# A Fourier mixing layer and two MLPs: where seven weight conversions and the split of x are placed

## The chip, the core and the metric

The kernel runs on one core of a Trainium2 chip. The metric is the device time of one execution in microseconds (us), lower is better. The inputs are float32 in HBM, and the output is float32.

## The reference, cut to what matters

```python
X = np.fft.rfft(x, axis=1)                       # x: (2, 3008, 256)
Yr = Xr @ w_r - Xi @ w_i + b_r                   # complex mixing, 256 x 256
Yi = Xr @ w_i + Xi @ w_r + b_i
Yr = np.sign(Yr) * np.maximum(np.abs(Yr) - 0.01, 0.0)   # and Yi
y = np.fft.irfft(Y, n=3008, axis=1).astype(np.float32)
for w_in, w_out, act in ((w_in1, w_out1, gelu_sigmoid), (w_in2, w_out2, silu)):
    y = act(y.reshape(6016, 256) @ w_in) @ w_out        # 256 x 2048, 2048 x 256
```

The weights of the two MLPs arrive as 64-bit patterns of doubles (the kernel reads them as int64) and have to be turned into float32 on the chip.

## The kernel before

The program has four stages that PE runs one after the other: the forward transform (16 groups of float32 matmuls, L344), the mixing (12 units, L496 to L502), the inverse transform (16 steps of float32 matmuls, L344 again) and the two MLPs (L727 and L755). Below, the units of the mixing are counted from 0 to 11: unit i is one (batch, parity, block), and its input x is two tiles of 128x512, `xt...0` and `xt...1` (cosine and sine part).

**The mixing.** Units 0 and 1 (`n32` is 2) use float32 matmuls. Units 2 to 11 are split: x is written as a high part `xh` (float32r, a CAST on ACT) and a low part `xl`, and each product takes three passes (high with high weight, high with low weight, low with high weight), 24 matmuls and one for the bias. The low part is made by ACT (it writes -x rounded, L476) and by a DMA that POOL issues and that adds x to it in place (L477). `xsplit` makes both parts, several units ahead. After a unit, `mid_post` (L506 on) copies a PSUM bank with ACT (`us`), adds and subtracts on DVE (`sd`), thresholds on ACT and DVE (`th`), and `mid_fold` makes the tiles `f` that the inverse reads, on DVE and POOL (`f`, `fb`, `fd`).

**A conversion** of a block of MLP weights goes through the engines in turn: a DMA of SP brings the raw bits into the one buffer `raw64`; ACT takes an absolute value (`cv_c`, L165); DVE does five steps (L170 to L174); a DMA that POOL issues adds `cv_c` to `cv_a` (L227; 256 KB); then the block is placed: for `wi` blocks DVE makes four sums `tmp` (L202 to L205), ACT casts two high parts (L99) and POOL subtracts two low parts (L100); for `wo` blocks one cast and one subtraction. `tick` does the next link of this chain for the next block, at the places that the lists `tf` (forward), `tm` (mixing) and `ti` (inverse) name. There are two buffers `cv_a`.

**What sets the order.** In the forward stage POOL and SP follow the written order, in the mixing SP, in the inverse PE; a scheduler orders the other engines' instructions at build time. Each engine then takes its list strictly in that order, and an instruction that waits holds up all behind it.

**Memory.** The `xt` slots (14 and 12) hold x and, once x is read, the tiles `f`. The pool `nh` on the left holds 8 low and 6 high parts. The pool `wib0` for weight blocks 4 and 5 (`wi4`, `wi5`) is opened on the left only after `nh` and `wh` are closed, at the end of the mixing.

```python
for i in range(N('n32') + 4):
    xsplit(i, 1)
    if i < N('n32') + 3:
        xsplit(i, 0)
for i in range(len(mids)):
    ps = mid_mm(i)
    if i >= N('n32'):
        xsplit(i + 4, 1)
        xsplit(i + 3, 0)
```

Of the kernel before, what the change touches and what calls it, by code (L numbers as in the profile page):

```python
# [21 lines left out]
P = 128  # L22
# [34 lines left out]
def spectral_mlp_kernel(ctx, tc, xin, mfwd, minv, wc, bias, w_in1, w_out1, w_in2, w_out2, outT):  # L57
# [360 lines left out]
    load_m()  # L418
    for g in range(3, N('fa')):
        fold(g)  # L420
    prev = None
    for g, (q, b, t) in enumerate(groups):
        fold(g + N('fa'))
        ps = fwd_mm(g)
        if b == B - 1 and m_order[0][0] == "f":
            load_m()
        if prev is not None:
            fwd_evac(*prev)
        prev = (g, ps)
        if g == 6:  # L430
            closed("lv0")
            wc_p = opened("wc", "right")
            wc_s = wc_p.tile([P, 2, 3 * D], F32, name="wc_s")
            bias_hl = wc_p.tile([P, 2 * D], F32R, name="bias_hl")
            bias_lo = wc_p.tile([1, 2 * D], F32R, name="bias_lo")
            bias_f = wc_p.tile([P, 2 * D], F32, name="bias_f")
            nc.gpsimd.memset(bias_f, 0.0)
            ones = wc_p.tile([P, P], F32R, name="ones")
            ones_f = wc_p.tile([P, P], F32, name="ones_f")

            neglam = wc_p.tile([P, 1], F32, name='neglam')
# [24 lines left out]
    xsp = {}

    def xsplit(i, part):
        if not N('n32') <= i < len(mids):
            return  # L470
        b, p, j = mids[i]
        for cs in range(2):
            x = xt[b, p, j, cs].rearrange("p q m c -> p (q m c)")
            if part:
                t = nh_p.tile([P, 512], F32R, tag="lo", name="xl", bufs=8)
                nc.scalar.mul(t, x, -1.0)  # L476
                nc.gpsimd.dma_start(out=t, in_=x, accum_op=ALU.add)  # L477
            else:
                t = nh_p.tile([P, 512], F32R, tag="hi", name="xh")
                nc.scalar.copy(t, x)  # L480
            xsp[b, p, j, cs, part] = t[:, :].rearrange("p (q m c) -> p q m c", q=2, m=2)
# [553 lines left out]
```

## Time and profile before

| | |
|---|---|
| median of 3 runs | 1181.35 us (1181.19 to 1182.56) |
| the profiled execution | 1181.88 us, of which its span is 1179.8 us |
| PE busy | 1157.4 us, 98% of the span |
| DVE, ACT, POOL busy | 632.7, 761.3, 499.9 us |
| mixing on PE | 67.3 to 140.4 us of the span |
| inverse on PE | 140.4 to 197.6 us |

PE is nearly always busy, so what a change can give or take lies in PE's few waits. The share of busy time hides them: they are read from PE's timeline, and what ended each of them from the names behind the arrow.

### The profile page before, as it was taken

The numbers are of one execution on the slowest core, as the hardware profiler recorded it, in microseconds if no ns is written. First come the engines' busy times: TensorE is split into PE (matmuls) and PEld (weight loads), VectorE is DVE, ScalarE is ACT, GpSimd is POOL, SyncE is SP. The second block draws the span as 40 slices with busy tenths as digits, with TensorE's granted clock in tenths as the row PEclk, the third lists the DMA queues.
The fourth block names the chain that finished last, engine by engine and source line by source line (L and its number), as shares of the span: only waits on it lengthen the run. The fifth ranks groups of instructions, "written<-read, shape, count | busy, mean of one in ns | idle before, by whom it ended". The sixth has DMA issues, their size and how long they took to land.

```text
span 1179.8 us, 14452 instructions
## 1 busy us (share of the span) xinstructions
PE 1157.4 (98%) x5036; PEld 940.4 (80%) x5036; DVE 632.7 (54%) x976; ACT 761.3 (65%) x1437; POOL 499.9 (42%) x421
## 2 busy tenths in 40 slices
PE   7999989999999999999999999999999999999998
PEld 4758866788888888888889978878888888888897
DVE  7857998666456465565564553432532623524422
ACT  2465633678667667677667776666765765766655
POOL 2353532454444444444436755333333333433333
PEclk9999999999999999999999999999999999999999
DMA  7568332231221221121120100000000000000000
GB/s 267 181 135 229 54 72 54 55 80 28 54 72 36 54 72 28 45 72 37 54 63 28 54 18 19 1 37 1 1 37 1 20 17 1 36 1 1 36 1 32
DMA packets 33610, 61.35 MB, mean 52 GB/s; under 512 B 3073, under 2 KB 12289, under 8 KB 33538
## 3 DMA queue, kind: packets, MB, share of 16 engines
q1 hardware_dynamic: 25730, 46.28, 11.6%
q0 software_dynamic: 7808, 14.16, 6.9%
q8 instruction: 39, 0.64, 0.2%
q14 instruction: 33, 0.27, 0.1%
HBM read 35.92 MB, written 10.35 MB: 39 GB/s over the span
## 4 chain that ended last, share of the span: by engine, by line
PE 72%; ACT 5%; DVE 2%; issue 1%; DMA 0%; POOL 0%; DVEq 0%; ACTq 0%; POOLq 0%
PE o L727 38%; PE x L755 34%; ACT yt L758 2%; ACT g L760 1%; ACT x L674 1%; DVE x L681 1%; ACT yt L774 0%; DVE yt L776 0%; DVE yt L731 0%; DVE yt L797 0%; ACT yt L791 0%; DMA cv_a<-cv_c 0%; ACT yt L789 0%; ACT yt L731 0%; ACT wi L99 0%
## 5 line engine op out<-in xcount | busy, mean ns | idle before, releaser
L765 POOL TENSOR_TENSOR g<-yt,g 128x512 fp32r<-128x512 f32 (+1 forms) x282 | 361.3, 1294 | 531.6 <-PE x L755 364.3
L727 PE MATMUL o<-g,wo 128*128 128x512 f32 (+1 forms) x2304 | 561.0, 386 | 0.9 <-POOL g L765 0.9
L755 PE MATMUL x<-x,wi 128*128 128x512 f32 (+1 forms) x2016 | 501.7, 387 | 5.4 <-ACT yt L791 2.0
L727 PEld LDWEIGHTS o<-g,wo 128*128 128x128 f32 x2304 | 432.4, 188 | 83.6 <-POOL g L765 1.2
L755 PEld LDWEIGHTS x<-x,wi 128*128 128x128 f32 x2016 | 376.0, 188 | 86.0 <-ACT yt L774 5.6
L758 ACT ACTIVATE yt<-yt 128x512 f32<-128x512 f32 (+1 forms) x288 | 179.1, 622 | 257.8 <-DVE yt L797 209.9
L760 ACT CAST g<-yt 128x512 fp32r<-128x512 f32 (+1 forms) x384 | 234.4, 612 | 11.8
L797 DVE TENSOR_TENSOR yt<-yt,x 128x512 f32<-128x512 f32 (+1 forms) x96 | 64.7, 674 | 212.9 <-PE x L755 212.6
L776 DVE TENSOR_TENSOR yt<-yt,x 128x512 f32<-128x512 f32 (+1 forms) x96 | 64.8, 675 | 168.7 <-ACT yt L774 165.9
L765 DVE TENSOR_TENSOR g<-yt,g 128x512 fp32r<-128x512 f32 (+1 forms) x102 | 72.7, 713 | 77.8 <-ACT g L760 77.8
L344 PE MATMUL psf<-m,xf 128*128 128x376 f32 (+2 forms) x208 | 61.1, 456 | 6.4 <-DVE xf L303 6.1
L681 DVE TENSOR_TENSOR x<-yt,x 128x512 fp32r<-128x512 f32 (+1 forms) x46 | 47.8, 1038 | 36.1 <-ACT x L674 36.1
L800 DVE TENSOR_TENSOR yt<-yt,x 128x512 f32<-128x512 f32 (+1 forms) x96 | 64.7, 674 | 0.0
L344 PEld LDWEIGHTS psf<-m,xf 128*128 128x128 f32 x208 | 39.2, 199 | 27.6 <-DVE xf L303 7.3
L774 ACT COPY yt<-x 128x512 f32<-128x512 f32 (+1 forms) x96 | 54.7, 570 | 5.9 <-issue 3.6
L758 ACT ACTIVATE yt<-x 128x512 f32<-128x512 f32 (+1 forms) x96 | 56.1, 584 | 2.1 <-PE x L755 2.1
L344 PE MATMUL psi<-m,f 128*128 128x376 f32 (+3 forms) x208 | 52.1, 406 | 4.3 <-DVE rt L374 4.3
L791 ACT COPY yt<-x 128x512 f32<-128x512 f32 (+1 forms) x96 | 55.8, 581 | 0.8 <-PE x L755 0.8
L789 ACT COPY yt<-x 128x512 f32<-128x512 f32 (+1 forms) x96 | 54.8, 571 | 0.8 <-PE x L755 0.8
L344 PEld LDWEIGHTS psi<-m,f 128*128 128x128 f32 x208 | 37.2, 194 | 17.8 <-DVE rt L374 5.5
L227 POOL DMA_DIRECT2D cv_a<-cv_c x32 | 27.8, 870 | 24.7 <-DVE cv_c L174 14.2
L384 ACT COPY xt<-psf 128x128 f32<-128x128 f32 (+2 forms) x96 | 18.6, 282 | 28.6 <-PE psf L344 28.5
(99 smaller groups left out, 817.8 us busy)
## 6 DMA issues: line engine op xcount, KB each, us to landing
raw<-in_wi SPq DMA_DIRECT2D x32, 256.0 KB, 3.2
cv_a<-cv_c POOLq DMA_DIRECT2D x32, 256.0 KB, 3.3
raw<-in_wo SPq DMA_DIRECT2D x16, 512.0 KB, 3.4
raw<-in_x SPq DMA_DIRECT2D x12, 512.0 KB, 4.8
xl<-xt POOLq DMA_DIRECT2D x20, 256.0 KB, 7.6
out_t<-yt SPq DMA_DIRECT2D x20, 256.0 KB, 2.0
m<-in_mf SPq DMA_DIRECT2D x4, 564.0 KB, 5.3
m<-in_mi SPq DMA_DIRECT2D x4, 564.0 KB, 10.5
```

The source lines that it names most:

```text
L344: nc.tensor.matmul(ps, hi[:, c : c + P], m[:, k, :w], start=i == 0, stop=i == last)
L681: E('xl1' if l else 'xl0' if i == 0 else 'xl', k).tensor_sub(lo, src, r32(hi))
L727: nc.tensor.matmul(acc[h, mm], st, mv, start=first and k == 0, stop=last and k == 2)
L755: nc.tensor.matmul(ps, st, mv, start=first and m == 0, stop=m == 2, skip_group_check=True)
L758: nc.scalar.activation(g, g if src is None else src, func)
L760: nc.scalar.copy(gh, g)
L765: eng.tensor_sub(gl, g, r32(gh))
L776: nc.vector.tensor_add(y1, y1, Y)
L789: nc.scalar.copy(y2, Z)
L791: nc.scalar.copy(y3, X)
L797: nc.vector.tensor_add(y2, y2, X)
L800: nc.vector.tensor_add(y3, y3, Z)
```

## The change

It does four things. The ticks of the mixing go from units 2, 6, 10 to units 1, 4, 7, 10 and those of the inverse from steps 1, 4, 7, 10 to 2, 5, 8. High parts of x are put into the `xt` slots, so that `nh` keeps low parts alone, 6 of them where 8 were. `wib0` is opened at the start of the mixing. The low parts of unit 2 get two tiles of their own in the pool `wc` and are made in the forward stage; those of the other units are made three units ahead, where it was four.

```diff
-'tm': [2, 6, 10], 'ti': [1, 4, 7, 10]
+'tm': [1, 4, 7, 10], 'ti': [2, 5, 8]
...
+    def xsplit(i, part, pool=None):
...
+            if part:
+                t = pool.tile([P, 512], F32R, tag="lo", name="xl", bufs=2 if pool is wc_p else None)
+                nc.scalar.mul(t, x, -1.0)
+                nc.gpsimd.dma_start(out=t, in_=x, accum_op=ALU.add)
+            else:
+                t = slot(cs, F32R, "xh")
+                nc.scalar.copy(t, x)
...
         if g == 13:
             prep_wc()
+            xsplit(N('n32'), 1, wc_p)
...
     mid_p = opened("mid", "right", 2)
     ft = {}
+    wib_p.append(opened("wib0", "left", 2))
     wh_p = opened("wh", "left")
-    nh_p = opened("nh", "left", N('nhb'))
+    nh_p = opened("nh", "left", 6)
...
-    for i in range(N('n32') + 4):
-        xsplit(i, 1)
-        if i < N('n32') + 3:
-            xsplit(i, 0)
+    for i in range(N('n32'), N('n32') + 3):
+        if i > N('n32'):
+            xsplit(i, 1, nh_p)
+        xsplit(i, 0)
     for i in range(len(mids)):
         ps = mid_mm(i)
         if i >= N('n32'):
-            xsplit(i + 4, 1)
+            xsplit(i + 3, 1, nh_p)
             xsplit(i + 3, 0)
...
     closed("mid", "wc", "nh", "wh")
-    wib_p.append(opened("wib0", "left", 2))
```

**The low parts of unit 6, on ACT.** The names: `us` is the copy of a unit's bank (`us_838` before and `us_835` now are unit 2's, `us_887` is unit 3's), `xt1000` and `xt1001` are x of unit 6, `wi4` is the fifth block. Before:

```order
L517 ACTIVATE th_770<-sd_766,neglam_379 128x512
L509 COPY us_838<-psm_723 128x512
L517 ACTIVATE th_770<-sd_766,neglam_379 128x512
L165 ACTIVATE cv_c_1227<-raw64_1030 128x512
L480 CAST xh_756<-xt0120_106 128x512
L476 ACTIVATE xl_750<-xt1000_108 128x512
L480 CAST xh_758<-xt0121_107 128x512
L476 ACTIVATE xl_753<-xt1001_109 128x512
L517 ACTIVATE th_844<-sd_840,neglam_379 128x512 x2
L509 COPY us_890<-psm_797 128x512
```

Now:

```order
L511 COPY us_835<-psm_742 128x512
L165 ACTIVATE cv_c_1088<-raw64_917 128x512
L436 CAST xh_879<-xt1010_110 128x512
L99 CAST wi4_1249<-cv_a_902 128x384
L99 CAST wi4_1249<-tmp_1250 128x512
L519 ACTIVATE th_841<-sd_837,neglam_379 128x512 x2
L511 COPY us_887<-psm_794 128x512
L432 ACTIVATE xl_821<-xt1000_108 128x512
L436 CAST xh_953<-xt1020_112 128x512
L436 CAST xh_881<-xt1011_111 128x512
L432 ACTIVATE xl_824<-xt1001_109 128x512
```

ACT reached `xl` of unit 6 before it turned to unit 2's thresholds (`th_844`); now it does so behind both casts of `wi4`, unit 2's thresholds (`th_841`) and unit 3's copy. Its tile is one that unit 3 reads, so it also waits for unit 3's matmuls.

**The DMAs of POOL for units 6 to 8.** Here `fd` is made of the folds of units 3 and 4. Before, from the DMA of the fifth conversion on:

```order
L227 DMA cv_a_1015<-cv_c_1014 128x512
L530 TENSOR_TENSOR f0011_836<-th_770 128x512
L477 DMA xl_750<-xt1000_108 128x512
L477 DMA xl_753<-xt1001_109 128x512
L477 DMA xl_824<-xt1010_110 128x512
L477 DMA xl_827<-xt1011_111 128x512
L227 DMA cv_a_1228<-cv_c_1227 128x512
L530 TENSOR_TENSOR f0101_940<-th_896 128x512
L477 DMA xl_876<-xt1020_112 128x512
L477 DMA xl_879<-xt1021_113 128x512
L536 TENSOR_TENSOR fd_995<-f0100_938,fb_993 128x512
```

Now, from the same place:

```order
L100 TENSOR_TENSOR wi4_1249<-tmp_1250,wi4_1249 128x512
L227 DMA cv_a_1089<-cv_c_1088 128x512
L433 DMA xl_821<-xt1000_108 128x512
L433 DMA xl_824<-xt1001_109 128x512
L100 TENSOR_TENSOR wi5_1387<-cv_a_1089,wi5_1387 128x384
L433 DMA xl_873<-xt1010_110 128x512
L433 DMA xl_876<-xt1011_111 128x512
L227 DMA cv_a_1252<-cv_c_1251 128x512
L100 TENSOR_TENSOR wi5_1387<-tmp_1388,wi5_1387 128x512
L532 TENSOR_TENSOR f0101_959<-th_893 128x512
L538 TENSOR_TENSOR fd_1014<-f0100_957,fb_1012 128x512
L433 DMA xl_947<-xt1020_112 128x512
```

Unit 6's low parts (`xt1000`, `xt1001`) left ahead of the sixth conversion's DMA and now leave behind it, and unit 8's (`xt1020`) left ahead of `fd` and now leave behind it.

**DVE in the inverse,** from one release of a PSUM bank that PE waits for (L374, batch 1, first step) to the next (L374, second step). Before:

```order
L374 TENSOR_TENSOR rt_1451<-psi_1401,eo_1452 128x4x94
L665 TENSOR_TENSOR yt_1325<-yt_1325 128x512
L627 TENSOR_TENSOR ac_1480<-rt_1451,psi_1456 128x377
L681 TENSOR_TENSOR x_1604<-tmp_1527,x_1603 128x512
L627 TENSOR_TENSOR ac_1480<-rt_1451,psi_1457 128x377
L619 TENSOR_TENSOR rt_1451<-psi_1441,eo_1466 128x2x2x95
L628 TENSOR_TENSOR rt_1451<-rt_1451,psi_1456 128x377
L683 TENSOR_TENSOR tmp_1527<-yt_1325,tmp_1527 128x512
L170 TENSOR_SCALAR cv_c_1489<-cv_c_1489 128x512
L628 TENSOR_TENSOR rt_1451<-rt_1451,psi_1457 128x377
L374 TENSOR_TENSOR rt_1451<-eo_1466,psi_1441 128x4x94
```

Now:

```order
L374 TENSOR_TENSOR rt_1451<-psi_1422,eo_1452 128x4x94
L666 TENSOR_TENSOR yt_1346<-yt_1346 128x512
L682 TENSOR_TENSOR x_1604<-tmp_1540,x_1603 128x512
L628 TENSOR_TENSOR ac_1494<-rt_1451,psi_1470 128x377
L684 TENSOR_TENSOR tmp_1540<-yt_1346,tmp_1540 128x512
L620 TENSOR_TENSOR rt_1451<-psi_1441,eo_1480 128x2x2x95
L629 TENSOR_TENSOR rt_1451<-rt_1451,psi_1470 128x377
L172 SCALAR_TENSOR_TENSOR cv_a_1461<-raw64_1405,cv_c_1460 128x512
L628 TENSOR_TENSOR ac_1494<-rt_1451,psi_1471 128x377
L374 TENSOR_TENSOR rt_1451<-eo_1480,psi_1441 128x4x94
```

Between the two releases stand eight steps where nine stood; ahead of the first of them, in the inverse, stood twelve more steps of conversions and sums, and now none.

## Rows read from the trace of the kernel before

**Rows 1.** Busy time by stretch: us, PE, PEld, DVE, ACT, POOL, granted clock, DMA share, GB/s.

```profile
83.60:140.40 56.80, 56.80 (x248) 46.62 (x249) 47.68 (x88) 35.51 (x62) 25.50 (x24) 1.00 0.73 165
140.40:163.10 22.70, 22.70 (x135) 21.60 (x133) 21.74 (x36) 8.01 (x15) 12.95 (x12) 1.00 0.17 41
...
167.80:171.40 3.60, 0.00 (x0) 0.00 (x0) 3.60 (x7) 2.15 (x4) 1.83 (x1) 1.00 0.19 34
171.40:175.70 4.30, 4.25 (x8) 2.37 (x9) 4.30 (x9) 0.00 (x0) 0.00 (x0) 0.62 0.00 0
```

**Rows 2.** PE's timeline: start, us, what; in brackets the wait and what ended it.

```profile
83.56 0.50 PE L499 MATMUL psm<-wh,xl 128*128 128x512 f32 x1 [1.46 <-DMA xl<-xt]
...
103.14 0.39 PE L502 MATMUL psm<-bias_hl,ones 128*128 128x512 f32 x1
...
108.85 0.39 PE L502 MATMUL psm<-bias_hl,ones 128*128 128x512 f32 x1
...
163.71 4.06 PE L344 MATMUL psi<-m,f 128*128 128x376 f32 x12 [0.59 <-DVE rt L374]
171.45 8.91 PE L344 MATMUL psi<-m,f 128*128 128x376 f32 x22 [3.68 <-DVE rt L374]
```

**Rows 3.** DVE's groups by line in the inverse, 140 to 198 us: the conversion's five steps.

```profile
L172 DVE SCALAR_TENSOR_TENSOR cv_a<-raw,cv_c 128x512 uint32<-128x512 uint32 x4 | 3.5, 879 | 0.0
L171 DVE TENSOR_SCALAR cv_c<-cv_c 128x512 uint32<-128x512 uint32 x3 | 2.8, 945 | 0.0
L174 DVE SCALAR_TENSOR_TENSOR cv_c<-raw,cv_c 128x512 f32<-128x512 uint32 x4 | 2.7, 683 | 0.0
...
L173 DVE TENSOR_SCALAR cv_c<-cv_a 128x512 uint32<-128x512 uint32 x4 | 2.5, 615 | 0.0
...
L170 DVE TENSOR_SCALAR cv_c<-cv_c 128x512 f32<-128x512 f32 x3 | 2.3, 782 | 1.0 <-ACT cv_c L165 1.0
```

**Rows 4.** ACT's timeline in the mixing: a raw block, units 2 and 3, unit 6's low part.

```profile
68.13 0.68 ACT L165 ACTIVATE cv_c<-raw 128x512 f32<-128x512 f32 x1 [3.60 <-DMA raw<-in_wi]
...
91.46 0.57 ACT L509 COPY us<-psm 128x512 f32<-128x512 f32 x1
...
95.09 0.63 ACT L476 ACTIVATE xl<-xt 128x512 fp32r<-128x512 f32 x1
...
100.90 0.57 ACT L509 COPY us<-psm 128x512 f32<-128x512 f32 x1
```

**Rows 5.** DVE's timeline in the mixing: conversions and the fold that `fd` waits for.

```profile
83.13 3.06 DVE L171 TENSOR_SCALAR cv_c<-cv_c 128x512 uint32<-128x512 uint32 x1
...
88.58 0.42 DVE L173 TENSOR_SCALAR cv_c<-cv_a 128x512 uint32<-128x512 uint32 x1
...
89.51 0.68 DVE L174 SCALAR_TENSOR_TENSOR cv_c<-raw,cv_c 128x512 f32<-128x512 uint32 x1
...
97.30 0.29 DVE L202 TENSOR_TENSOR tmp<-cv_a 128x128 f32<-128x128 f32 x1 [3.15 <-DMA cv_a<-cv_c]
...
115.63 0.69 DVE L530 TENSOR_TENSOR fb<-th 128x512 f32<-128x512 f32 x1
```

**Rows 6.** POOL's timeline in the mixing: weight steps, `fd`, and the low parts behind it.

```profile
83.26 1.40 POOL L100 TENSOR_TENSOR wi<-cv_a,wi 128x384 fp32r<-128x384 f32 x1
84.24 1.66 POOL L100 TENSOR_TENSOR wi<-tmp,wi 128x512 fp32r<-128x512 f32 x1
...
107.56 1.80 POOL L530 TENSOR_TENSOR f<-th 128x512 f32<-128x512 f32 x1 [1.44 <-DVE th L518]
...
116.41 1.68 POOL L536 TENSOR_TENSOR fd<-f,fb 128x512 f32<-128x512 f32 x1 [5.33 <-DVE fb L530]
```

**Rows 7.** DMA issues, KB each, us to landing; around 90.7, 96.0 and 118.0 us.

```profile
cv_a<-cv_c POOLq DMA_DIRECT2D x1, 256.0 KB, 6.5
...
xl<-xt POOLq DMA_DIRECT2D x1, 256.0 KB, 8.9
...
xl<-xt POOLq DMA_DIRECT2D x1, 256.0 KB, 3.8
```

More of the change, by code (lines that the diff above doesn't have):

```diff
@@ L10 @@
 F32 = mybir.dt.float32
-CFG = {'lv0': 'V', 'lv': 'VVVVVPVVVVVP', 'dd0': 'VPVVPPPPPVVP', 'dd': 'VVVVVVVVVVPV', 'ths': 'VVVVPV', 'thf': 'VVVP', 'ivf': 'VVVPVVVV', 'cva': 'P', 'pol': 'PPPP', 'pil': 'P', 'mvl': 'PVVP', 'xl': 'V', 'xse': 'V', 'gl': 'VPPPPPPP', 'tf': [6, 9, 12], 'tm': [2, 6, 10], 'ti': [1, 4, 7, 10], 'kb': [0, 1, 1, 1, 1, 1, 1, 0], 'kr': [0, 1, 0, 1, 0, 1, 1, 0], 'fa': 3, 'xp': [2, 4, 4, 5], 'xq': [1, 4, 1], 'xs': 4, 'xi': [11, 12, 13, 15], 'xsi': 9, 'ca': 4, 'tl': True, 'fwd': 'Pool,SP', 'rest0': 'all', 'rest1': 'all', 'last1': 'all', 'inv': 'PE', 'mid': 'SP', 'last0': 'all', 'thm': 'A', 'gl0': 'PVPVVVPV', 'gl2': 'PPPPPPPP', 'gl3': 'PPPPPPPV', 'xl0': 'V', 'xl1': 'V', 'pre': 14, 'pre2': 0, 'yd': 6, 'lvb': 6, 'mlp': 'none', 'pr': 'VVVP', 'pf': 'PV', 'eo': '0010', 'n32': 2, 'xa': 4, 'nhb': 6, 'ddb': 6, 'mlp1': 'all', 'mlp2': 'all'}
+CFG = {'lv0': 'V', 'lv': 'VVVVVPVVVVVP', 'dd0': 'VPVVPPPPPVVP', 'dd': 'VVVVVVVVVVPV', 'ths': 'VVVVPV', 'thf': 'VVVP', 'ivf': 'VVVPVVVV', 'cva': 'P', 'pol': 'PPPP', 'pil': 'P', 'mvl': 'PVVP', 'xl': 'V', 'xse': 'V', 'gl': 'VPPPPPPP', 'tf': [6, 9, 12], 'tm': [1, 4, 7, 10], 'ti': [2, 5, 8], 'kb': [0, 1, 1, 1, 1, 1, 1, 0], 'kr': [0, 1, 0, 1, 0, 1, 1, 0], 'fa': 3, 'xp': [2, 4, 4, 5], 'xq': [1, 4, 1], 'xs': 4, 'xi': [11, 12, 13, 15], 'xsi': 9, 'ca': 4, 'tl': True, 'fwd': 'Pool,SP', 'rest0': 'all', 'rest1': 'all', 'last1': 'all', 'inv': 'PE', 'mid': 'SP', 'last0': 'all', 'thm': 'A', 'gl0': 'PVPVVVPV', 'gl2': 'PPPPPPPP', 'gl3': 'PPPPPPPV', 'xl0': 'V', 'xl1': 'V', 'pre': 14, 'pre2': 0, 'yd': 6, 'lvb': 6, 'mlp': 'none', 'pr': 'VVVP', 'pf': 'PV', 'eo': '0010', 'n32': 2, 'xa': 4, 'nhb': 6, 'ddb': 6, 'mlp1': 'all', 'mlp2': 'all'}
 NUM = dict(li=[5, 6, 7, 8], n32=2, nhb=6, tf=[5, 9, 13], tm=[1, 3, 5, 7, 9, 11], ti=[0, 2, 4, 6, 8, 10, 12, 14, 14, 15, 15], kb=[2] * 8, kr=1, fa=3, fe=2, pm=0, nf=4, lvb=6, ddb=8, ivb=1, eob=1, fsb=6, f1=3, f2=0, fm=[7, 8, 9], fi=[1, 1, 2, 2], pre=13, pre2=1, yd=3, psh=0, ie=[12], xp=[1, 3, 4, 5], xq=[1, 2, 2], xs=5, nw=4, xi=[14, 14, 15, 15], xsi=13, rw=2, ca=4, cc=2, tb=1, tmn=1)
@@ L420, in spectral_mlp_kernel @@
         fold(g)
+    xsp = {}
+    mids = [(b, p, j) for b in range(B) for p in range(2) for j in range(NJ)]
+    def xsplit(i, part, pool=None):
+        if i >= len(mids):
+            return
+        b, p, j = mids[i]
+        for cs in range(2):
+            x = xt[b, p, j, cs].rearrange("p q m c -> p (q m c)")
+            if part:
[5 more added lines that the diff above has]
+                nc.scalar.copy(t, x)
+            xsp[b, p, j, cs, part] = t[:, :].rearrange("p (q m c) -> p q m c", q=2, m=2)
     prev = None
@@ L452, in spectral_mlp_kernel @@
             tick(N('tf').count(g))
-    mids = [(b, p, j) for b in range(B) for p in range(2) for j in range(NJ)]
     closed("xs", "lv", "raw", "m0")
@@ L465, in spectral_mlp_kernel @@
     nc.vector.tensor_sub(wl, wc_s, r32(wh))
[L466 to L481, printed above, removed]
     def mid_mm(i):
```

## The prediction

> **What bounds the kernel now.** I read the table by stretch first. In the mixing PE is busy for 56.80 of 56.80 us, in the first part of the inverse for 22.70 of 22.70 [rows 1]: PE is the bound, and a change pays only where PE waits. Then PE's timeline, for those waits. From the mixing to the end of the inverse there are three: 1.46 us for a DMA of low parts (unit 2's, the first split unit) and 0.59 and 3.68 us for DVE's release of a PSUM bank in the inverse [rows 2]. Then the granted clock. Behind the 3.6 us in which PE does nothing stands a stretch of 4.3 us with a mean of 0.62 [rows 1], so PE, at the lower of its two levels (1.2 GHz) for most of it, lost 0.38 x 4.3 = 1.6 us more. What makes DVE late there: it is busy for 21.74 of 22.70 us and then for every microsecond of the wait [rows 1], and 18 conversion steps, 13.8 us, are among its work in the inverse [rows 3].
>
> So the waits that the change can end come to 1.46 + 0.59 + 3.68 + 1.6 = 7.3 us, and with all of it and nothing against it the profiled execution of 1181.9 us would be 1174.5 us.
>
> **The change, part by part.**
>
> *Unit 2's low parts in the forward stage.* Their two ACT steps and two DMAs go about 14 us ahead of their use; ACT waits for PE for much of the forward stage, and three groups of banks lie between a copy and its reuse. They cost nothing there; if that cover were gone, it would be two ACT steps of 0.63 us [rows 4]. Gain: 1.46 us. What is late next is unit 2's second high part: its slot is one that unit 0 reads, and on ACT it stands behind a cast of the third weight block. I estimate that it is ready at 81 us, against a need at 82.5 us; its bounds are no wait and the old 1.46 us.
>
> *Conversions out of the inverse.* `wi4` and `wi5` can now be placed in the mixing, since `wib0` is open. In the order, twelve DVE steps leave the inverse ahead of the first bank release that PE waited for, and one of nine leaves between the two. By the page's means these twelve are worth 12 x 13.8/18 = 9.2 us if all were conversion steps; four are shorter sums, so I say 8. That is more than 0.59 + 3.68 us, and both waits should go, and the slow clock with them: 5.9 us. Bounds: 0, if DVE reaches the inverse late by as much, and 5.9 us.
>
> *What it adds to the mixing.* About ten DVE steps, four casts on ACT, four weight steps on POOL (1.40 to 1.66 us each [rows 6]). DVE has 56.8 - 47.7 = 9.1 us to spare there [rows 1], so the sum of the work fits. What doesn't fit is where it stands: in front of the low parts.
>
> *Low parts three units ahead, in six tiles.* A unit lasts 108.85 - 103.14 = 5.71 us [rows 2]. Unit 6's bias is at 108.85 us, the thirteenth matmul at 0.23 us each; its low part is the third, so at 106.5 us, and without the 1.46 us at 105.1 us. When does it land? In the trace ACT made it at 95.09 us, between its copies of unit 2 (91.46) and unit 3 (100.90) [rows 4]. In the change it stands behind the copy of unit 3 and behind `wi4`'s casts; on POOL its DMA stands behind that of the sixth conversion, which needs that conversion's last DVE step. The fifth conversion's last DVE step ended at 90.2 us [rows 5]. Its predecessors in the change are the same raw block, which lands no earlier than the 68.13 us of the trace [rows 4], and the same chain; I find 89. From there: a DMA of 6.5 us while the inverse's matrices load [rows 7], which DVE waits for as it did in the trace until 97.30 [rows 5]: 95.6. Then seven steps of the next conversion and of the sums, unit 2's three `sd`, two more conversion steps and a threshold, 5 us by their spacing: 101. POOL issues that conversion's DMA and then, at 102, the low part. The nearest rows for its landing are 8.9 us with the loads and 3.8 us without [rows 7]; the loads start just then, and I take 7.5: 109.5. PE waits 109.5 - 105.1 = 4.4 us, and I add 1.6 us for the clock, as in the inverse. Bounds: nothing (the chain 4 us earlier), and 8 us.
>
> Unit 8 checks this by another way. Its low part now stands behind `fd`. In the trace `fd` ended at 116.41 + 1.68 = 118.1 us, right behind `fb` at 115.63 [rows 5, 6]. In the change two more POOL steps stand ahead of it and DVE has some 2 us more of conversions by then; I say 120.5. With 3.8 us [rows 7] it lands at 124.3. PE needs it at 105.1 + 2 x 5.71 = 116.5 us. So by unit 8 PE is 7.8 us late, whatever part of it it has waited before. Units 9 to 11 follow without a further wait: their DMAs leave behind unit 8's, 0.9 us apart, and each has a unit's time more. Cost of the mixing: 8 us, between 0 (POOL reaching it at PE's own pace) and 13 (both chains 5 us later).
>
> *SP's queue.* The inverse's first matrices now stand behind one more raw block, the others behind the first `wo` block; they are needed only from the end of the mixing on, past 138 us. Nothing.
>
> *The sum.* 1181.9 - 1.46 - 5.9 + 8.0 = 1182.5 us for the profiled execution, which is 0.5 us above the median of the runs shown: **1182.0 us** against 1181.35.
>
> **A row and a rule.** One single-input DVE step of 128x512 took 3.06 us [rows 5] while POOL's two weight steps ran beside it, from 83.26 to 85.90 [rows 6]; by the page its means in the inverse are 0.62 to 0.95 us [rows 3]. Four such POOL steps move into the stretch where DVE's chain decides; I charged them in the 5 us and 2 us above with little. The Trainium skill ("SBUF — State Buffer", Who interferes with whom) says that a DVE operation with two inputs or in a two-port mode and a POOL operation shut each other out for a whole instruction; by that rule each of the four would be paid in full. The trace agrees for that step, not always: beside POOL's fold at 107.56 us it was POOL that took 1.80 us.
>
> **The rivals.**
>
> *A, the forecast: the gain is eaten.* Mixing 5 to 10 us longer, inverse 5.9 us shorter: 1179.0 to 1184.0 us. For: ACT's and POOL's order, and a chain that in the trace too waited for its DMAs (3.15 us at 97.30). Against: ACT is rid of eight pairs of splits ahead of unit 0's copy, and the chain could run earlier.
>
> *B, faster: the low parts arrive.* If the fifth conversion ends by 86 us and the sixth's DMA doesn't wait for the loads, unit 6 waits for nothing and unit 8 for 2 to 4 us. Mixing up to 5 us longer: 1174.0 to 1179.0, the middle 1176.5. For: each link needs only 2 us. Against: unit 8's `fd`.
>
> *C, slower: POOL's weight steps shut DVE out.* By the row above a pair of them costs DVE 3.06 - 0.42 = 2.6 us (0.42 is the length of a like step two later [rows 5]), and two pairs lie on the chain: 5.3 us more, mixing 13 us longer, 1187.3 us. It decides from 2.4 us on, one pair. For: the 3.06. Against: at 97 to 104 us DVE waits for its DMAs anyway, and a step that waits loses nothing.
>
> *D: the change doesn't do what it says.* DVE enters the inverse late, the bank waits stay, and the mixing pays as in A: 1188.
>
> **How the numbers follow.** A 0.36, B 0.32, C 0.25, D 0.07. What a measurement of this kernel can tell from no change is about 0.2%, 2.4 us: A lies within it, B below, C and D above. So faster 0.32, same 0.36, slower 0.32. The range from 1175.5 to 1188.0 us leaves out the full gain of B and the far end of C and D; A's own is 1179.0 to 1184.0.
>
> **What would show it.** In the profile after: no wait at unit 2; a wait of PE for the DMA of `xl` of 3 to 8 us at unit 6, and another at unit 7 or 8; a granted clock under 1 behind the longer one; the end of the mixing at 145 to 149 us, where it was 140.4; no wait over 1 us for DVE in the inverse, which takes 51 us, where it took 57. If the mixing ends by 141 us, my chain of conversions is too slow and B holds. If it ends past 150 us, and DVE steps beside POOL's `wi` steps take 2 to 3 us, it is C.

## The result, and the profile after

The changed kernel took **1190.83 us** (median of 6 runs, 1189.43 to 1191.90) where the kernel before took 1181.27 us in the same comparison: a ratio of 1.0081, interval [1.0068, 1.0094], or 9.6 us slower. That is above the whole range of the prediction. The stages of the two profiled executions, by the places of PE's first matmul of each:

| | forward | mixing | inverse | MLPs to the end | span |
|---|---|---|---|---|---|
| before | 67.27 | 73.14 | 57.18 | 982.21 | 1179.8 |
| after | 67.17 | 88.59 | 50.69 | 982.25 | 1188.7 |

So all of the difference lies in two stages: the mixing is 15.45 us longer and the inverse 6.49 us shorter.

**The one long wait.** PE's timeline of the changed kernel (start, us, what; in brackets the wait and what ended it) has a single wait over 0.3 us from the mixing to the end of the inverse:

```profile
119.07 0.79 PE L501 MATMUL psm<-wh,xl 128*128 128x512 f32 x1 [14.19 <-DMA xl<-xt]
```

It is the third matmul of unit 6, which needs that unit's first low part. It was due at 119.07 - 14.19 = 104.88 us. The wait at unit 2 and both waits for DVE in the inverse [rows 2] are gone. The table by stretch (us, PE, PEld, DVE, ACT, POOL, granted clock, DMA share, GB/s) gives what came after the wait:

```profile
104.88:119.07 14.19, 0.00 (x1) 0.01 (x1) 10.45 (x22) 7.86 (x14) 5.88 (x7) 0.61 0.76 213
119.07:123.00 3.93, 3.93 (x9) 3.13 (x10) 3.90 (x9) 3.01 (x6) 1.93 (x3) 0.50 1.10 264
123.00:126.00 3.00, 3.00 (x10) 2.35 (x9) 2.67 (x4) 2.07 (x5) 3.00 (x3) 0.67 1.08 281
67.17:155.76 88.59, 74.40 (x285) 55.32 (x284) 66.68 (x117) 47.86 (x91) 37.30 (x36) 0.90 0.63 146
155.76:206.45 50.69, 50.69 (x226) 38.73 (x224) 45.81 (x74) 14.84 (x28) 15.87 (x12) 1.00 0.18 42
```

Behind the wait PE ran at a granted clock of 0.50 (the lower of its levels, 1.2 GHz) and then of 0.67: 0.50 x 3.93 + 0.33 x 3.00 = 3.0 us more. 14.19 + 3.0 - 1.46 = 15.7 us, against 15.45 measured. The last row has PE busy for the whole inverse.

**Why the low part came so late.** DVE's timeline in the mixing shows the ends of the fourth, fifth and sixth conversions (L174) and what held them:

```profile
75.50 1.76 DVE L484 TENSOR_TENSOR wl<-wc_s,wh 128x1536 fp32r<-128x1536 f32 x1 [2.98 <-ACT wh L483]
77.17 0.69 DVE L172 SCALAR_TENSOR_TENSOR cv_a<-raw,cv_c 128x512 uint32<-128x512 uint32 x1
...
79.64 0.68 DVE L174 SCALAR_TENSOR_TENSOR cv_c<-raw,cv_c 128x512 f32<-128x512 uint32 x1
...
85.89 0.29 DVE L202 TENSOR_TENSOR tmp<-cv_a 128x128 f32<-128x128 f32 x1 [4.11 <-DMA cv_a<-cv_c]
...
87.11 1.24 DVE L170 TENSOR_SCALAR cv_c<-cv_c 128x512 f32<-128x512 f32 x1
...
89.41 1.78 DVE L172 SCALAR_TENSOR_TENSOR cv_a<-raw,cv_c 128x512 uint32<-128x512 uint32 x1
...
92.77 0.69 DVE L174 SCALAR_TENSOR_TENSOR cv_c<-raw,cv_c 128x512 f32<-128x512 uint32 x1
...
100.40 0.29 DVE L202 TENSOR_TENSOR tmp<-cv_a 128x128 f32<-128x128 f32 x1 [3.46 <-DMA cv_a<-cv_c]
...
101.14 1.11 DVE L204 TENSOR_TENSOR tmp<-tmp,cv_a 128x128 f32<-128x128 f32 x1
102.17 1.51 DVE L171 TENSOR_SCALAR cv_c<-cv_c 128x512 uint32<-128x512 uint32 x1
...
106.70 0.68 DVE L174 SCALAR_TENSOR_TENSOR cv_c<-raw,cv_c 128x512 f32<-128x512 uint32 x1
```

The fifth conversion ended at 93.5 us and the sixth at 107.4; before, the fifth ended at 90.2 [rows 5]. Three things can be read off. `wl`, which waits for ACT, stands inside the fourth conversion, and the raw buffer is free only behind its L174 (79.64, ended at 80.3; before, the fourth conversion ended at 72.9). Twice DVE stands at the sums of one block (L202) until that block's DMA has landed, with the next conversion's steps queued behind. And four steps that last 0.28 to 0.69 us elsewhere take 1.11 to 1.78 us (87.11, 89.41, 101.14, 102.17). The first of the four ends a little behind POOL's step at 86.89, the second behind that at 89.28, and so on. POOL's timeline shows what ran beside these steps, and the order in which the DMAs left:

```profile
86.89 1.17 POOL L100 TENSOR_TENSOR wi<-cv_a,wi 128x384 fp32r<-128x384 f32 x1 [3.83 <-ACT wi L99]
89.28 1.36 POOL L100 TENSOR_TENSOR wi<-tmp,wi 128x512 fp32r<-128x512 f32 x1 [1.22 <-ACT wi L99]
...
100.93 1.17 POOL L100 TENSOR_TENSOR wi<-cv_a,wi 128x384 fp32r<-128x384 f32 x1 [5.71 <-DVE tmp L203]
102.07 1.33 POOL L532 TENSOR_TENSOR f<-th 128x512 f32<-128x512 f32 x1
...
107.91 0.88 POOL L227 DMA_DIRECT2D cv_a<-cv_c  x1 [2.02 <-issue]
108.49 2.08 POOL L433 DMA_DIRECT2D xl<-xt  x2
```

SP's queue, at the same moment, and the DMA issues of 108.45 to 109.2 us (KB each, median us to landing):

```profile
107.44 0.38 SPq L156 DMA_DIRECT2D raw<-in_wo  x1
107.86 2.09 SPq L127 DMA_DIRECT2D m<-in_mi  x4
```

```profile
m<-in_mi SPq DMA_DIRECT2D x2, 564.0 KB, 9.4
cv_a<-cv_c POOLq DMA_DIRECT2D x1, 256.0 KB, 8.3
xl<-xt POOLq DMA_DIRECT2D x1, 256.0 KB, 10.5
```

The last four loads of the inverse's matrices stand behind the raw block of tick 7, so the first of them left 0.6 us ahead of the low part and the others beside it, and it took 10.5 us to land.

The chain was late from its first link. ACT took the raw block of the fourth conversion at 70.93 us, where it had taken it at 68.13 [rows 4], and ACT's cast `wh` (73.92, for which `wl` waits) stands behind that step:

```profile
70.93 0.67 ACT L165 ACTIVATE cv_c<-raw 128x512 f32<-128x512 f32 x1 [5.57 <-DMA raw<-in_wi]
```

The two DMAs of that raw block took 7.5 us to land, where before they had taken 4.1. In the new order POOL issued the DMAs of eight low parts (units 2 to 5) together, at the end of the forward stage, beside that block:

```profile
60.42 7.09 POOL L433 DMA_DIRECT2D xl<-xt  x8
```

No run moved these eight alone, so that they slowed the raw block is likely but not shown.

### The profile page after: what moved, and what is told of

Its sections match the earlier page's. It is cut to its first block, busy times and chain, and to the rows that moved or that the text cites. A ratio compares the mean times of both kernels' runs of the same rounds, so it can differ in the third digit from the quotient of the medians.

```text
span 1188.7 us, 14458 instructions
## 1 busy us (share of the span) xinstructions
PE 1157.3 (97%) x5036; PEld 941.6 (79%) x5036; DVE 634.6 (53%) x976; ACT 761.4 (64%) x1437; POOL 497.6 (42%) x421
## 4 chain that ended last, share of the span: by engine, by line
PE 72%; ACT 5%; DVE 2%; issue 1%; DMA 0%; POOL 0%; DVEq 0%; ACTq 0%; POOLq 0%
PE o L728 38%; PE x L756 34%; ACT yt L759 2%; ACT g L761 1%; ACT x L675 1%; DVE x L682 0%; ACT yt L775 0%; DVE yt L777 0%; DVE yt L732 0%; DVE yt L798 0%; ACT yt L792 0%; DMA cv_a<-cv_c 0%; ACT yt L790 0%; ACT yt L732 0%; ACT wi L99 0%
## 5 line engine op out<-in xcount | busy, mean ns | idle before, releaser
L501 PE MATMUL psm<-wh,xl 128*128 128x512 f32 x80 | 32.4, 405 | 14.2 <-DMA xl<-xt 14.2
L227 POOL DMA_DIRECT2D cv_a<-cv_c x32 | 30.3, 947 | 19.9 <-issue 7.2
```

## The experiments

Fourteen kernels ran, each compared with the kernel before on the same chip; the table has those whose stages are set side by side. Mixing, its waits and the inverse are those of the one profiled execution, in us; waits under 0.3 us are left out.

| run | ratio to before, interval | mixing | PE's waits in it | inverse | both |
|---|---|---|---|---|---|
| before | 1 | 73.14 | 1.46 | 57.18 | 130.32 |
| the change | 1.0081 [1.0068, 1.0094] | 88.59 | 14.19 | 50.69 | 139.28 |
| last loads later | 1.0072 [1.0057, 1.0087] | 86.45 | 11.42 | 52.28 | 138.73 |
| loads early | 1.0060 [1.0042, 1.0079] | 85.28 | 10.50 | 52.04 | 137.32 |
| eight tiles | 1.0044 [1.0029, 1.0059] | 85.00 | 8.60 | 50.68 | 135.68 |
| eight tiles, loads early | 1.0032 [1.0018, 1.0045] | 73.01 | 0.78 | 58.37 | 131.38 |
| old ticks | 1.0073 [1.0058, 1.0088] | 87.39 | 13.44 | 52.34 | 139.73 |
| `wl` on POOL | 1.0086 [1.0066, 1.0105] | 85.28 | 10.68 | 52.44 | 137.72 |
| before, unit 2's part | 1.0016 [1.0004, 1.0027] | 72.40 | 0.48 | 57.93 | 130.33 |
| before, `wi4` and `wi5` on DVE | 0.9989 [0.9980, 0.9998] | 73.03 | 1.42 | 55.34 | 128.37 |

### What the 14.2 us are made of

**The last four loads of the inverse's matrices, later.**

```diff
+CFG = {'li': [5, 6, 10, 10], ...
-        if i in N('li'):
+        for _ in range(N('li').count(i)):
             load_m()
```

> The changed kernel with one thing moved: the last four loads of the inverse's matrices go behind the second wo block on SP's queue (tick 10) where they went behind the first. The orders of ACT, DVE and POOL are unchanged up to unit 6's low parts. By the theory that the loads slow the landing, the low part leaves at 108.5 us as before and lands after 4 to 6 us where it took 10.6: PE waits 8 to 9.5 us, and the time is 1184 to 1186 us. By the theory that the place in the queues is all, it lands at 118 to 119 us as before, PE waits 13 to 14 us, and the time is 1190 to 1191 us.

The low part left behind the same conversion's DMA, at 109.73 us in an execution whose forward stage ended 1.9 us later, and took 5.4 us; the wait shrank by 6.1 us to 8.13. Here are the DMA issue and PE's waits:

```profile
xl<-xt POOLq DMA_DIRECT2D x2, 256.0 KB, 5.4
```

```profile
114.94 0.80 PE L501 MATMUL psm<-wh,xl 128*128 128x512 f32 x1 [8.13 <-DMA xl<-xt]
...
132.79 0.50 PE L501 MATMUL psm<-wh,xl 128*128 128x512 f32 x1 [2.20 <-DMA xl<-xt]
...
135.55 0.50 PE L501 MATMUL psm<-wh,xl 128*128 128x512 f32 x1 [1.09 <-DMA xl<-xt]
```

So the loads were worth about 5 us of the landing. The time was 1188.45 us, not the 1184 to 1186 of the theory: the moved loads, which now left from 121.44 us on, then stood beside the low parts of a later unit (one that left at 123.35 took 9.4 us to land; PE waited 2.20 and 1.09 us), and the inverse was 1.6 us longer.

**All eight loads early.** The same loop with `'li': [1, 1, 1, 1]`.

> The changed kernel (six tiles, three units ahead) with all eight loads of the inverse's matrices directly behind the raw block of tick 1 on SP's queue; nothing else is edited. The scheduler then places unit 6's first low part behind the first weight step of wi4 and ahead of the sixth conversion's DMA. If the depth is the larger part, unit 6 still waits, because the low part follows unit 3's copy on ACT: 3 to 8 us, 1183 to 1187 us. If the loads are the larger part, the wait is under 3 us and the time is that of the run with both, 1183 to 1184 us.

1187.00 us, against 1179.52 for before beside it. The first two waits, 1.84 and 1.37 us, are unit 6's; four more of 0.50 to 2.76 us follow at later units. The long stall is cut into pieces, and their sum stays at 10.5 us: with six tiles low parts come just in time or late at one unit after the other. Two things changed here, not one: in the new order unit 6's low parts also left ahead of the sixth conversion's DMA (103.13 and 105.86 us, against 107.43), so this run does not price the loads alone; the run above does.

**Eight tiles, four units ahead.** Unit 2's two tiles join the rotation.

```diff
-            xsplit(i + 3, 1, nh_p)
+            xsplit(i + 4, 1, wc_p if i % 4 == 2 else nh_p)
```

> The changed kernel with low parts four units ahead again: units 6 and 10 take the two tiles that unit 2 leaves, so eight tiles rotate in place of six, with no more memory. By the theory that the depth decides (three units ahead in six tiles puts unit 6's low part behind both casts of wi4, unit 3's copy and the sixth conversion), the low part of unit 6 now leaves POOL at 101 to 104 us, ahead of the sixth conversion's DMA, where it left at 108.5, and lands at 106 to 109: PE waits 1 to 5 us at unit 6 where it waited 14.2, and the time is 1177 to 1181 us. By the theory that the loads of the inverse's matrices decide (they are issued at 107.9 us), the wait falls only if the DMA is clear of them; issued at 101 to 104 it lands in 5 us, so the two agree here. By the theory that POOL's weight steps holding up DVE decide, the conversion chain is as late as before and the wait stays above 8 us: 1185 us or more.

1186.01 us against 1180.55. Unit 6 waited 1.35 us, as worked out; but unit 7 waited 6.73 and 0.52. In this order unit 6's low parts left at 103.11 us, ahead of the sixth conversion's DMA, and it is unit 7's that stand behind it: they left at 108.79, 0.6 us after the same loads. The place behind that DMA, not the unit, carries the wait. The time missed the 1177 to 1181 us of the depth alone; the chain of conversions was as late as before (the sixth ended at 107.7 us, 107.4 in the changed kernel), as the third theory had it.

**Both together.**

> Both: eight rotating tiles, four units ahead, and all eight loads of the inverse's matrices directly behind the raw block of tick 1 on SP's queue (from some 81 us on, in a stretch where the DMA engines were nearly idle from 79 to 94 us). Unit 6's low parts now stand directly behind the fifth conversion's DMA on POOL (94 us). By the theories of depth and of loads they land by 101 us, PE needs them at 104.8, and no unit waits: the mixing ends at 138 to 139 us, the inverse takes 50.7 us, and the time is 1172.5 to 1175 us. By the theory that POOL's weight steps holding up DVE decide, a wait of over 3 us remains and the time is 1178 us or more.

No wait in the mixing was longer than 0.48 us, and it took 73.01 us, 0.1 less than before. So with depth and loads both put right the whole stall is gone. But the time was 1183.51 us, not the 1172.5 to 1175 expected, and 0.32% slower than before: PE now waited seven times in the inverse, 5.8 us in sum. Four of the waits:

```profile
145.14 1.57 PE L344 MATMUL psi<-m,f 128*128 128x192 f32 x8 [0.70 <-ACT us L511]
...
147.38 2.21 PE L344 MATMUL psi<-m,f 128*128 128x192 f32 x12 [0.68 <-DVE sd L515]
...
157.20 4.81 PE L344 MATMUL psi<-m,f 128*128 128x192 f32 x28 [1.05 <-DVE rt L374]
...
174.47 9.74 PE L344 MATMUL psi<-m,f 128*128 128x376 f32 x30 [1.43 <-DVE rt L374]
```

DVE's groups by line in the inverse say why. This is the group L513, the first of a unit's three `sd` steps, of the changed kernel and then of this one:

```profile
L513 DVE TENSOR_TENSOR sd<-us,psm 128x512 f32<-128x512 f32 x1 | 0.7, 680 | 0.0
```

```profile
L513 DVE TENSOR_TENSOR sd<-us,psm 128x512 f32<-128x512 f32 x3 | 2.0, 679 | 0.0
```

Without the stall, DVE came into the inverse with three units' work left, where the changed kernel (and the kernel before) has one. Neither edit does this by itself: with eight tiles alone the inverse took 50.68 us, with early loads alone 52.04, and in both the mixing still stalled.

**The tick lists of the kernel before** (`'tm': [2, 6, 10], 'ti': [1, 4, 7, 10]`), all else as changed.

> The changed kernel with the tick lists of the kernel before (mixing 2, 6, 10 and inverse 1, 4, 7, 10); the tiles, pools and depth of the change stay. By the theory that the depth decides, unit 6's low part still stands behind unit 3's copy and the sixth conversion's DMA, so PE waits 8 to 14 us at unit 6: 1185 to 1191 us. By the theory that the fourth conversion in the mixing decides, the wait goes below 4 us and the time is 1177 to 1182 us.

1189.20 us and a wait of 11.92 us at unit 6. So the stall does not need the new tick lists; the rest of the change (tiles, depth, `wib0` opened early) is enough. It does not need the loads either: here they left from 95.70 to 100.5 us and the low part landed in 5.2 us, but the sixth conversion's DMA left 3.0 us later than in the changed kernel (110.92 us, against 107.91).

**`wl` made by POOL.**

```diff
-    nc.vector.tensor_sub(wl, wc_s, r32(wh))
+    nc.gpsimd.tensor_sub(wl, wc_s, r32(wh))
```

> The changed kernel with one step on another engine: POOL makes wl (L484), which on DVE stood between the second and the third step of the fourth conversion and waited for ACT's cast of wh; nothing else is edited. By the theory that this place is what makes the chain late, the fourth conversion ends at 73 to 76 us where it ended at 80.3, the fifth at 83 to 87 where it ended at 93.5, the sixth before 98 where it ended at 107.4, and unit 6's low part leaves POOL by 100: PE waits 0 to 5 us at unit 6 where it waited 14.2; the time is 1179 to 1184 us, not lower, because DVE then enters the inverse late. By the theory that the chain is held by its DMAs and POOL's steps, the fifth conversion ends after 91 us and PE waits over 9 us: 1187 us or more.

1188.40 us. The fourth, fifth and sixth conversions ended 2.7, 4.3 and 2.3 us earlier than in the changed kernel, the low part left POOL at 106.19, and PE waited 8.22 us for it. DVE's timeline:

```profile
88.48 0.68 DVE L174 SCALAR_TENSOR_TENSOR cv_c<-raw,cv_c 128x512 f32<-128x512 uint32 x1
...
97.20 0.29 DVE L202 TENSOR_TENSOR tmp<-cv_a 128x128 f32<-128x128 f32 x1 [3.30 <-DMA cv_a<-cv_c]
...
104.39 0.68 DVE L174 SCALAR_TENSOR_TENSOR cv_c<-raw,cv_c 128x512 f32<-128x512 uint32 x1
```

Neither theory held alone. How much of the lateness is `wl` itself this run does not show: the raw block of the fourth conversion also came to ACT 2.25 us earlier (68.68 us, against 70.93), and on POOL `wl` took 3.43 us where it had taken 1.76 on DVE, and the fourth conversion then waited for it. The rest of the chain did not catch up: DVE again stood 3.30 us for a conversion's DMA with the next one's steps behind it, and steps beside POOL's were stretched again (98.01, 99.04 and 102.74 us: 1.10, 1.51 and 1.13 us). PE also waited 2.02 us in this unit for DVE's `sd`, which it had not before, and the time was no better than the changed kernel's (ratios 1.0086 and 1.0081).

### Whether the inverse's gain stands without the stall

**Unit 2's part alone, on the kernel before:** its low parts in two tiles of `wc` made in the forward stage, the other units in six, four units ahead as before.

> The kernel before with one part of the change alone: unit 2's low parts in two tiles of the pool wc, made in the forward stage; units 6 and 10 take these tiles later, so that eight tiles rotate four units ahead as before; high parts, conversions and tick lists stay. By my theory this part is worth the 1.46 us of the wait at unit 2 and costs nothing, if DVE is not later in the inverse: 1178.5 to 1180 us. By the theory that DVE's lateness sets the end of the inverse whatever PE does in the mixing, the 1.5 us come back as longer waits for the bank releases there: 1180 to 1181 us, no difference.

The wait at unit 2 was gone, and the time was no better: 1182.63 us against 1181.02, ratio 1.0016. In the profiled execution (1180.99 us, below the median) the mixing was 0.74 us shorter and the inverse 0.75 us longer. Its waits for DVE were all there, and the slow clock behind the long one cost more:

```profile
163.02 4.06 PE L344 MATMUL psi<-m,f 128*128 128x376 f32 x12 [0.42 <-DVE rt L374]
170.76 27.50 PE L344 MATMUL psi<-m,f 128*128 128x376 f32 x78 [3.68 <-DVE rt L374]
```

```profile
170.76:175.00 4.24, 4.24 (x7) 2.50 (x8) 4.24 (x9) 0.00 (x0) 0.00 (x0) 0.50 0.00 0
175.00:180.00 5.00, 5.00 (x15) 2.88 (x15) 5.00 (x9) 0.62 (x1) 0.00 (x0) 0.90 0.00 0
```

0.50 x 4.24 + 0.10 x 5.00 = 2.6 us, where before it was 1.6.

**Four conversions in the forward stage**, three runs: on the kernel before (`'tf': [5, 8, 11, 14], 'tm': [4, 9]`), on the run above (the same lists), and on the change with eight tiles and early loads (`'tf': [5, 8, 11, 14], 'tm': [3, 6, 9], 'li': [3, 3, 3, 3]`). They were to take work from DVE in the mixing and the inverse.

> The kernel before with one conversion moved out of the mixing into the forward stage (ticks 5, 8, 11, 14 there, 4 and 9 in the mixing, the inverse's as they were); nothing else. By the theory that DVE's work from the start of the mixing to the end of the inverse (110 us in 130 us) sets the end of the inverse, the 5 conversion steps and 4 sums less (some 4 us) shorten mixing and inverse together by 1.5 to 4 us, from 130.3 to 126.5 to 129 us, as long as the forward stage doesn't grow (DVE is busy for 49.7 of its 67.3 us): 1177.5 to 1180 us. By the theory that only the steps inside the inverse count, its 18 conversion steps are all still there, the waits of 0.59 and 3.68 us stay, and the time is within 1 us of before.

> The same ticks as the run with four conversions in the forward stage, and unit 2's low parts made in the forward stage. By the theory of DVE's work the 1.46 us of the wait at unit 2 now come back in full or in part, because DVE is no longer the last to arrive: 0.5 to 1.5 us below the run without unit 2's part. By the theory that the inverse's own steps decide, the two runs are equal.

> The changed kernel with eight rotating tiles, early loads of the inverse's matrices, and four conversions in the forward stage (5, 8, 11, 14), three in the mixing (3, 6, 9) and three in the inverse (2, 5, 8), so that six are in mixing and inverse where seven were. By the theory of DVE's work mixing and inverse together take 125 to 128 us where the run with seven took 131.4, DVE enters the inverse at most one unit behind (three sd steps left, where nine were left), and the time is 1176 to 1180 us. If the place of the conversions alone decided, this run and the one with seven would be equal, 1183 to 1184 us.

All three missed, and leave the question where it was: 1191.36, 1189.28 and 1186.57 us, ratios 1.0091, 1.0070 and 1.0048. The forward stage grew from 67.3 us to 71.8, 70.8 and 72.7, so the condition under which the first two were worked out did not hold. In the first, PE waited for DVE inside it:

```profile
49.94 21.98 PE L344 MATMUL psf<-m,xf 128*128 128x376 f32 x80 [3.32 <-DVE xf L303]
```

In the third, DVE entered the inverse two units behind, not three, and the inverse was 3.0 us shorter than with both edits alone (55.36); but the mixing was 3.1 us longer (76.10), with a wait of 1.90 us for ACT's `xh`, and both stages together took the same (131.46, against 131.38).

### POOL's steps beside DVE

**The `wi` subtractions (L100) on DVE,** `'pil': 'V'` for `'P'`: first on the change with eight tiles and early loads, then on the kernel before.

> The kernel with eight tiles and early loads, with the subtractions of the wi and wo... of the wi blocks' low parts (L100) on DVE in place of POOL. In the run before this one DVE took 63.4 us in the mixing and entered the inverse two units behind (nine sd steps left where the changed kernel leaves three). By the theory that POOL's steps hold DVE up, 22 steps that stretch to 0.8 to 1.8 us fall back to their 0.28 to 0.69 us: DVE gains some 5 us in the mixing and pays 4 x 1.2 us for the subtractions of wi2 to wi5, so it comes out 0 to 3 us ahead, POOL's queue is shorter by 1.2 us per step, and the time is 1180 to 1183.5 us. By the theory that only the amount of DVE's work counts, the added 5 us put it further behind: 1186 to 1189 us.

1183.37 us against 1181.02, ratio 1.0014 [0.9999, 1.0030], where it was 1.0032 [1.0018, 1.0045] with POOL: not worse, with seven more steps (6.2 us) on DVE in the mixing. The 16 sums there took 4.5 us where they had taken 7.8, and mixing and inverse together took 131.23 us where they had taken 131.38. That speaks for the theory that POOL's steps hold DVE up; but the intervals overlap, and no time was gained.

> The kernel before with the subtractions of the wi blocks' low parts (L100) on DVE in place of POOL, and nothing else edited; the scheduler then places the conversions a little earlier. By the theory that POOL's steps hold DVE up (in the inverse of the kernel before 18 conversion steps took 13.9 us where their undisturbed lengths make 9.5), the waits for the bank releases in the inverse fall by 1 to 3 us: 1178 to 1180 us. By the theory that only the amount of DVE's work counts, they grow: 1182 to 1185 us.

1182.84 us, ratio 1.0020 [1.0008, 1.0033]: slower. The inverse did get shorter, 54.26 us. But the scheduler had put a conversion's DMA among the first low parts, and the mixing had waits of 0.76, 1.12 and 1.11 us (75.21 us in all); in the MLPs, where blocks are placed as well, PE waited 1.59 and 0.92 us for DVE at places where it had not.

So the next run moved **the four subtractions of `wi4` and `wi5` alone,** all at the start of the inverse.

```diff
-'pil': 'P'
+'pil': 'PPPPVVPP'
```

> The kernel before with the subtractions of the low parts of wi4 and wi5 alone (four steps, all at the start of the inverse) on DVE in place of POOL. The mixing is unchanged. By the theory that POOL's steps hold DVE up, the conversion steps and sums in the inverse, which took 13.9 and 2.2 us, get shorter by 2 to 4 us for 2.4 us of added work; with all blocks on DVE the inverse took 54.3 us where it took 57.2, and here it takes 54 to 56: 1178 to 1180 us, and the MLPs don't pay. By the theory of the amount of DVE's work, the inverse takes 58 to 60 us: 1182 to 1184 us.

**1177.62 us** against 1179.06 beside it, ratio 0.9989 [0.9980, 0.9998]: the one version that comes out ahead of the kernel before, by 0.1%, at the edge of what can be told. The inverse took 55.34 us with one wait of 2.43 us for DVE, where there were 0.59 and 3.68 [rows 2]. The wait that is left is the first one, and longer; the second is gone. DVE's timeline from the first release (L374) to the second, before and then in this run:

```profile
163.12 0.54 DVE L374 TENSOR_TENSOR rt<-psi,eo 128x376 f32<-128x376 f32 x1
163.57 2.46 DVE L665 TENSOR_TENSOR yt<-yt 128x512 f32<-128x512 f32 x1
...
168.99 1.49 DVE L170 TENSOR_SCALAR cv_c<-cv_c 128x512 f32<-128x512 f32 x1
...
170.86 0.53 DVE L374 TENSOR_TENSOR rt<-eo,psi 128x376 f32<-128x376 f32 x1
```

```profile
164.92 0.54 DVE L374 TENSOR_TENSOR rt<-psi,eo 128x376 f32<-128x376 f32 x1
165.38 0.68 DVE L665 TENSOR_TENSOR yt<-yt 128x512 f32<-128x512 f32 x1
...
169.47 0.54 DVE L374 TENSOR_TENSOR rt<-eo,psi 128x376 f32<-128x376 f32 x1
169.92 0.42 DVE L170 TENSOR_SCALAR cv_c<-cv_c 128x512 f32<-128x512 f32 x1
```

POOL's timeline of the kernel before, beside the two long steps:

```profile
163.53 1.94 POOL L100 TENSOR_TENSOR wo<-cv_a,wo 128x512 fp32r<-128x512 f32 x1
...
168.37 1.83 POOL L100 TENSOR_TENSOR wo<-cv_a,wo 128x512 fp32r<-128x512 f32 x1 [2.89 <-ACT wo L99]
```

Counted from the start of the inverse, the first release came 1.8 us later than before: four subtractions (2.5 us) were added ahead of it, and the two steps that POOL's subtractions had stretched (L172 and L518 at 143 to 145 us, 1.47 and 1.48 us, now 0.69 each) gave 1.6 us back. The second release came 1.35 us earlier, because between the two L665 was not stretched and L170 had moved behind the release. What had stretched these two are subtractions of `wo` blocks, which stay on POOL in this run and only fall elsewhere (160.48 and 171.10 us). So in this execution the gain came from where steps met in the new order, not from the moved subtractions themselves, which took more than they gave back.

The Trainium skill ("SBUF — State Buffer", Who interferes with whom) says that the two engines exclude each other for a whole instruction when both want the ports that they share. The trace agrees for L665: 2.46 us beside POOL's step, 0.68 us with none beside it.

**The same with unit 2's part.**

> The same with unit 2's low parts made in the forward stage. If DVE is no longer the last to arrive in the inverse, the 1.46 us at unit 2 now count: mixing 71.7 to 72.4 us and inverse 54 to 56, 1176.5 to 1179 us. If DVE still is, mixing and inverse together are as without unit 2's part.

1179.65 us, ratio 1.0002 [0.9990, 1.0013]: the expected gain did not come, and unit 2's part again made nothing better. Its profiled execution, 1182.11 us, is among the longest of its twelve runs (1177.00 to 1182.30). In it PE waited 0.58, 1.05 and 1.11 us in the mixing and 3.93 us for DVE in the inverse. Why the part costs 2.0 us by the medians on top of the other edit stays open.

## Why the prediction was wrong, point by point

- **The likeliest case was the right mechanism, with its largest term mis-sized.** "PE waits 109.5 - 105.1 = 4.4 us": the need was right (104.88), the landing was 119.07. The place was right too, behind the sixth conversion's DMA on POOL and unit 3's copy on ACT.
- **The step that failed is the chain of conversions.** For the fifth I wrote "the same chain; I find 89"; it ended at 93.5. It was not the same chain: the fourth conversion's raw block came to ACT 2.8 us later than in the trace before, `wl` had moved into that conversion (L172 at 77.17), the raw buffer came free at 80.3, and two steps were stretched by 1.9 us beside POOL's `wi` steps. From there to the sixth conversion's end I took 12 us, and it took 13.9; stretched steps are 1.9 us of that again. Together 6.4 us. The second half was too short in itself: with `wl` on POOL the fifth ended at 89.2, as I had it, and the sixth still at 105.1, where I had 101. I had read ACT's and POOL's order for unit 6 and DVE's for the inverse, but not DVE's for the fourth conversion.
- **The landing: 7.5 us taken, 10.5 measured.** Both bounds (8.9 and 3.8) came from other positions among the loads; here the first of the last four loads left 0.6 us ahead. The run with them later put the landing at 5.4 us. I had put SP's queue at nothing, because its loads are needed late; what they cost is what they do to the low part beside them, 5.1 us here.
- **The clock: 1.6 us taken, 3.0 measured.** Behind the 14.19 us of nothing the granted clock was 0.50 for 3.9 us and 0.67 for 3.0 more; behind the 3.68 us, from which I took the price, it was 0.62 for 4.3.
- **Unit 8** had no wait of its own: PE came 17 us late to it. What I said of it ("whatever part of it it has waited before") held, but unit 6 alone exceeded it.
- **Unit 2's wait** went, as forecast. It is no gain by itself: alone on the kernel before, the inverse gave 0.75 us back, and the ratio was 1.0016.
- **"Both waits should go, and the slow clock with them: 5.9 us"** was right in size (6.49) and wrong as a term of its own. I added it to the mixing's cost as if the two were independent. With the stall taken away, the inverse took 58.37 us, longer than before. In the five other runs with a mixing of 85 us or more it took 50.7 to 52.4 us. DVE used the stall to catch up: it was busy for 10.45 us of the 14.19. "The sum of the work fits" was the wrong test. DVE is busy for 110.2 us in the two stages of the kernel before, 112.5 in the changed one and 111.0 in the run without the stall: the change only moves its work.
- **The rivals.** C named something that is there, POOL's steps stretching DVE's: 3.8 us of stretch lie on the chain from 85.9 to 107.4 us, 1.1 of it beside a fold and not a `wi` step, for the 5.3 that C gave two pairs. That these would come off PE's wait is read from the trace; no run took POOL's steps alone off the changed kernel. Of C's signs the mixing's end past 150 us came (155.76), the steps of 2 to 3 us did not (1.1 to 1.8). I had C as another way than A, and it was a part of A. Of D, DVE late in the inverse is what the run without the stall showed, but with a clean mixing. B was out from the fifth conversion on.

Seen as a sum, the prediction took the mixing as 6.5 us longer and the inverse as 5.9 us shorter; it was 15.45 and 6.49.

## What to carry to other kernels

A term that ends a wait in a later stage and one that adds a wait in an earlier stage are not independent when one engine feeds both: ask what the engine does while PE stands, and cost the case without the stall too. Before a low part or an operand is put at shorter notice, follow its queue back through every engine of the chain ahead of it, in the new order, and look which bulk loads leave at the same moment. Where two engines hold each other up, moving a few short steps changes which of the others meet: read the gain from the releases that PE waits for, one by one, and not from sums of busy time over the stage.

## What the runs showed of the hardware that was not expected

The length of a wait alone did not tell what it costs in clock. One of 2.43 us in the inverse brought the granted clock to 0.51 for the next 3.5 us, while one of 2.76 us in the mixing left it at 1.00 for as long (and the 1.46 us at unit 2 did too). These are the rows behind the two, of the run with `wi4` and `wi5` on DVE and of the run with early loads; the second contains a further wait of 1.35 us:

```profile
165.51:169.00 3.49, 3.49 (x6) 2.04 (x7) 3.49 (x7) 0.48 (x1) 0.64 (x1) 0.51 1.05 231
```

```profile
122.70:126.20 3.50, 2.15 (x8) 1.50 (x9) 3.50 (x7) 1.14 (x3) 1.54 (x2) 1.00 1.05 234
```

And a DMA of 256 KB that adds one tile to another in place took 5.4 us or 10.5 us to land at the same point of the program, by whether four loads of 564 KB left beside it, the first 0.6 us ahead.
